# A normaliser that goes through DRAM: sixteen rows in place of eight

## The chip, the cores and the metric

The kernel runs on one core of a Trainium2 chip. The core has a matrix engine (TensorE, PE in the profile), a vector engine (VectorE, DVE), a scalar engine (ScalarE, ACT), GpSimd (POOL), and SyncE (SP), which here only issues transfers; the transfers themselves run on 16 DMA engines. The metric is the device time of one launch in microseconds (us). Several launches are timed and their median is taken.

## The reference

The input x is 2048 tokens by 512 features in bf16. Four layers follow one another, each added to x behind a layer norm: A, B, A, B.

```
q, k, v = split(layernorm(x) @ wqkv)                     # 32 heads of 16
A:  phi(u) = concat(softmax(u @ w_phi), softmax(-u @ w_phi))   # 32 features per head
    kv = sum over tokens of phi(k) (x) v,   z = sum over tokens of phi(k)
    o  = (phi(q) @ kv) / (phi(q) . z + 1e-6)
B:  o  = softmax over 8 earlier positions (step 2) of q.k / 4, applied to v
x = x + o @ wo
```

The change is in layer A. The query's features phi(q) are softmaxes, and the result is divided by a denominator: for each token, head and sign one number, the normaliser rho, carries the reciprocal of the softmax sum and the reciprocal of the denominator. The kernel multiplies the unnormalised exponentials of the query by it.

## The kernel before

The 2048 tokens are four blocks (b = 0 to 3) of 512 tokens; a block is four tiles (t) of 128. L = 0 and 1 is the pair of layers A and B. For each L the kernel runs `s_a1` (keys and values of layer A) and `s_a2` (queries) for the four blocks, `s_akv` (the summed kv), and then for each block `s_a3` (denominator and normaliser), `s_a4` (output, projection, residual and next layer norm), and `s_b1`, `s_b2`, `s_b3` for layer B.

Each step of a stage is put on a list of its engine, and a long written-out order (`_ORDER`, L57) says in which sequence the steps of all stages are emitted. Each engine takes its instructions strictly in that order, and so does SP: a transfer that has to wait holds up all transfers behind it on SP. Semaphores of the program stand wherever one engine needs another's result. Transfers take their completion semaphores from eight in turn.

In `s_a3` the engines make rho: the products with the denominators on PE (`md`), a product and a sum on DVE (`dr`, L790 and L793), a logarithm and an exponential on ACT (`ln`, L796 and L797), and rho itself on DVE (`rho`, L801). It is a tile of 128 partitions: 32 rows (heads) for each of the four token tiles, with two signs (s) of 128 tokens each. The exponentials `Eq` of the query, however, have a head's 16 features on 16 partitions, eight heads to a group of 128 partitions, so that each value of rho has to reach 16 partitions. For four of the eight blocks this is done by matmuls with a 0/1 matrix (`bc`, L808) and DVE products from PSUM (`mulp`, L816). For the other four, listed in `_OPT["rho_dma"]` as (0,2), (0,3), (1,2) and (1,3), it is done by DMA:

- `wr` (L824) writes rho to a DRAM buffer `rd` of 8 rows and two signs, one row for each head within a group; a row holds 16 pieces (four token tiles by four head groups) of 128 values, that is 4 KB.
- `rdb(s)` (L831), once for each sign, reads each of the 8 rows sixteen times, so that each of the 128 partitions of the tile `Prho` receives 4 KB: 512 KB in all.
- `muld(s)` (L835) is one DVE product of `Eq` and `Prho`, 128 by 2048 values, in place.

SP's order around the four places is: the write, the two reads, and then whatever transfer comes next. At block (0,3) the transposing transfer `xnT<-xn` (L451), which brings the layer-normed block (0,2) to layer B's projections on PE (L927), stands between the two reads. Behind the reads come the loads of the values' tiles, `Vg<-V` (L988), which DVE multiplies by the attention weights (`pav`, L1081).

Of the kernel before, what the change touches and what calls it, by code (L numbers as in the profile page):

```python
# [8 lines left out]
BF16 = mybir.dt.bfloat16  # L9
# [7 lines left out]
P = 128  # L17
# [112 lines left out]
class _Fast:  # L130
# [640 lines left out]
    def s_a3(self, L, b, dma):  # L771
        nc, add = self.nc, self.step
        st = "a3_%d%d" % (L, b)
        zm = self.ZM[L]
        T = {}
# [42 lines left out]
        pitch = (16 + _OPT["rho_pad"]) * P  # L818

        def wr():  # L820
            self.RD[L, b] = rd = self.dram.tile([8, 2, pitch], BF16, name="rd%d%d" % (L, b))
            a = rd[0:1, 0, 0:P]
            dst = bass.AP(a.tensor, a.offset, [[P, 16], [2 * pitch, 8], [pitch, 2], [1, P]])
            nc.sync.dma_start(out=dst, in_=T["rho"][:])  # L824

        def rdb(s):
            rd = self.RD[L, b]
            T["P", s] = pr = self.med([4, NB, P], "Prho")
            a = rd[0:1, s, 0:P]
            src = bass.AP(a.tensor, a.offset, [[2 * pitch, 8], [0, 16], [1, 16 * P]])  # L830
            nc.sync.dma_start(out=pr[:].rearrange("p t a i -> p (t a i)"), in_=src)  # L831

        def muld(s):
# [14 lines left out]
        if dma:  # L848
            add(st, "SP", wr)
            for s in range(2):  # L850
                add(st, "SP", rdb, s)
            for s in range(2):
                add(st, "DVE", muld, s)
            return
# [963 lines left out]
```

## Time and profile before

| what | value |
|---|---|
| median of 3 runs | 330.01 us (329.47 to 330.12) |
| span of the profiled execution, first to last instruction | 327.5 us |
| PE, DVE, ACT busy | 95%, 92%, 85% of the span |
| SP's queue (q1) | 36816 packets, 34.81 MB |
| HBM read, written | 10.50 MB, 2.36 MB |
| granted TensorE clock | 0.998 |

For the profiled execution the trace has the span alone, and no device time; the runs' median is 2.5 us above the span. A row of the timeline gives the start in us from the span's first instruction, the duration, engine, line, operation and tile; in brackets stands how long the engine was idle before and what ended that wait. A row of the windows gives a stretch of time, each engine's busy time in it with the number of instructions, the granted clock, the mean share of the 16 DMA engines that moved a packet (it can come out above 1 where an engine overlaps packets), and the rate in GB/s. The profile's own name for a transfer's issue is the line on SPq.

### The profile page before, as it was taken

What the parts mean: (1) busy time and instruction counts of PE and PEld (TensorE: products, weight loads), DVE (VectorE), ACT (ScalarE), POOL (GpSimd) and SP (SyncE); (2) the same over time, 40 slices, a digit from 0 to 9 for tenths busy, and PEclk for the clock granted to TensorE, in tenths of its full rate; (3) what the DMA queues carried; (4) which work ended last, traced back from release to release, by engine and by line L of the source; (5) the groups of instructions that cost most, each with busy time, mean ns of one, the idle gap of its engine ahead of it and who ended that gap; (6) DMA issues with size and microseconds to landing.
All of it is one profiled execution on the core that took longest, in us unless ns stands there. A gap on an engine that the chain in (4) does not pass through costs nothing. (4 is left out here: it accounts for less than half of the span.)

```text
span 327.5 us, 8033 instructions
## 1 busy us (share of the span) xinstructions
PE 310.3 (95%) x3176; PEld 149.5 (46%) x3203; DVE 302.2 (92%) x439; ACT 279.3 (85%) x634; POOL 25.3 (8%) x50
## 2 busy tenths in 40 slices
PE   7999999999999999999999999979999999999873
PEld 3655456445444444443444455644544454433221
DVE  7998995998998999899999999699999999999993
ACT  5999988998888999989999999798999996676550
POOL 4000000000021003000000000000000208400000
PEclk9999999999999999999999999999999999999999
DMA  7980000004556899998750300023436977679952
GB/s 197 380 197 3 0 2 4 2 20 120 105 148 135 152 164 133 139 121 154 137 135 1 67 3 2 4 59 90 128 58 125 179 146 134 150 139 158 166 176 92
DMA packets 37388, 35.41 MB, mean 108 GB/s; under 512 B 23008, under 2 KB 32224, under 8 KB 37344
## 3 DMA queue, kind: packets, MB, share of 16 engines
q1 hardware_dynamic: 36816, 34.81, 53.6%
q8 instruction: 27, 0.44, 0.6%
q14 instruction: 17, 0.14, 0.2%
q10 hardware_dynamic: 528, 0.02, 0.1%
HBM read 10.50 MB, written 2.36 MB: 39 GB/s over the span
## 5 line engine op out<-in xcount | busy, mean ns | idle before, releaser
L927 PE MATMUL ps<-xnT,WB 128*128 128x512 bf16 x384 | 87.6, 380 | 0.5 <-DMA xnT<-xn 0.5
L1081 DVE TENSOR_TENSOR pav<-PT,Vg 128x4096 bf16<-128x4096 bf16 (+1 forms) x34 | 72.0, 2162 | 1.5 <-DMA Vg<-V 1.0
L1019 DVE TENSOR_TENSOR prod<-QT,K 128x4096 bf16<-128x4096 bf16 x32 | 72.5, 2291 | 0.3 <-ACT QT L192 0.2
L927 PEld LDWEIGHTS <-WB 128*128 128x128 bf16 x384 | 42.3, 114 | 43.3 <-issue 5.8
L520 PEld LDWEIGHTS <-oT 128*128 128x128 bf16 x256 | 23.8, 97 | 34.5 <-ACT oT L192 5.7
L192 ACT CAST oT<-ps 128x512 bf16<-128x512 f32 (+1 forms) x60 | 32.1, 587 | 8.4 <-PE ps L1090 7.1
L706 ACT ACTIVATE Eq<-ps 128x512 bf16<-128x512 f32 x64 | 34.0, 615 | 0.7 <-PE ps L698 0.6
L520 PE MATMUL ps<-WoB,oT 128*128 128x512 bf16 x122 | 32.1, 380 | 2.4 <-ACT oT L192 2.0
L599 ACT ACTIVATE Ek<-ps 128x512 bf16<-128x512 f32 x64 | 33.6, 622 | 0.4 <-PE ps L593 0.2
L698 PE MATMUL ps<-xnT,WA 128*128 128x512 bf16 x128 | 30.7, 380 | 0.6 <-DVE Eq L816 0.6
L540 ACT ACTIVATE sqd<-x 128x512 bf16<-128x512 bf16 x48 | 30.1, 643 | 1.0 <-DVE x L533 0.8
L605 PE MATMUL ps<-WA,xnT 128*128 128x512 bf16 x120 | 30.0, 380 | 0.5 <-issue 0.2
L593 PE MATMUL ps<-WA,xnT 128*128 128x512 bf16 x124 | 29.7, 380 | 0.6 <-DMA xnT<-xn 0.2
L520 PE MATMUL ps<-WoA,oT 128*128 128x512 bf16 x120 | 29.2, 380 | 0.4
L533 DVE SCALAR_TENSOR_TENSOR x<-ps,x 128x512 bf16<-128x512 f32 x38 | 25.4, 686 | 1.9 <-PE ps L520 1.7
L192 ACT CAST V<-ps 128x512 bf16<-128x512 f32 x31 | 17.5, 595 | 4.4 <-PE ps L927 4.3
L192 ACT CAST K<-ps 128x512 bf16<-128x512 f32 x31 | 17.8, 585 | 3.7 <-PE ps L927 3.3
L530 ACT ACTIVATE x<-ps 128x512 bf16<-128x512 f32 x26 | 15.1, 598 | 6.4 <-PE ps L523 6.3
L192 ACT CAST QT<-ps 128x512 bf16<-128x512 f32 x29 | 17.1, 592 | 2.5 <-PE ps L927 2.5
L651 DVE TENSOR_TENSOR Ek<-Ek,rk 128x4096 bf16<-128x4096 bf16 (+1 forms) x10 | 18.6, 1858 | 0.5 <-ACT rk L646 0.5
L593 PEld LDWEIGHTS <-xnT 128*128 128x128 bf16 x128 | 12.1, 97 | 15.4 <-DMA xnT<-xn 0.7
L446 ACT ACTIVATE xn<-x,nmr,rstd 128x512 bf16<-128x512 bf16 x23 | 18.2, 822 | 1.0 <-DVE nmr L435 0.8
(129 smaller groups left out, 433.3 us busy)
## 6 DMA issues: line engine op xcount, KB each, us to landing
Vg<-V SPq DMA_DIRECT2D x128, 131.5 KB, 4.4
Prho<-rd SPq DMA_DIRECT2D x8, 512.0 KB
x<-in_A_x_dram SPq DMA_DIRECT2D x3, 512.0 KB
WB<-in_B_wqkv_dram SPq DMA_DIRECT2D x3, 512.0 KB, 11.6
wraw<-in_A_wqkv_dram SPq DMA_DIRECT2D x4, 256.0 KB, 4.5
out_dram<-x SPq DMA_DIRECT2D x4, 256.0 KB, 2.2
out_dram<-x SPq DMA_DIRECT2D x8, 128.0 KB, 2.2
x<-in_A_x_dram SPq DMA_DIRECT2D x4, 128.0 KB
```

What stands on the lines that cost most here:

```text
L192: self.nc.scalar.copy(out=out, in_=in_)
L520: nc.tensor.matmul(y[:], lhsT=oT[:, c, t * P:(t + 1) * P], rhs=Wo()[:, c, :], start=(c == 0), stop=(c == NB - 1 and not onpe))
L533: nc.vector.scalar_tensor_tensor(out=xb[:, t, :], in0=T[t][:], scalar=1.0, in1=xb[:, t, :], op0=ALU.mult, op1=ALU.add, **kw)
L540: nc.scalar.activation(out=sqd[:], in_=xb[:, t, :], func=ACT.Square, accum_out=T["ss"][:, t:t + 1])
L593: nc.tensor.matmul(pk[:], lhsT=xnT[:, t, k, :], rhs=self.WA[:, k, D:2 * D], start=(k == 0), stop=(k == NB - 1))
L599: nc.scalar.activation(out=T["E"][:, t, s, :], in_=T["k", t][:], func=ACT.Exp, scale=1.0 - 2.0 * s)
L605: nc.tensor.matmul(pv[:], lhsT=xnT[:, t, k, :], rhs=self.WA[:, k, 2 * D:3 * D], start=(k == 0), stop=(k == NB - 1))
L698: nc.tensor.matmul(pq[:], lhsT=self.WA[:, k, hb * P:(hb + 1) * P], rhs=xnT[:, :, k, :], start=(k == 0), stop=(k == NB - 1))
L706: nc.scalar.activation(out=self.Eq[L, b][s][:, :, hb, :], in_=T[hb][:].rearrange("p (t i) -> p t i", t=4), func=ACT.Exp, scale=1.0 - 2.0 * s)
L927: nc.tensor.matmul(pp[:], lhsT=self.WB[:, k, i * D + c:(i + 1) * D:NB], rhs=xnT[:, :, k, :], start=(k == 0), stop=(k == NB - 1))
L1019: nc.vector.tensor_tensor(out=pr[:], in0=QT[:, c:c + 1, :].to_broadcast([P, NW, TB]), in1=win, op=ALU.mult)
L1081: nc.vector.tensor_tensor(out=pv, in0=PT[:, :, lo:lo + n].unsqueeze(1).to_broadcast([P, NB, 2, n]), in1=vw, op=ALU.mult)
```

## The change

The DRAM buffer gets 16 rows: each of the 8 old rows stands in it twice, one copy beside the other. Two transfers write it, one for each sign, where one transfer wrote both signs; each writes its 64 KB half of the new buffer with rho's values read twice (the repeat is a zero step in the source's access pattern). Each read then goes through 16 rows and reads each eight times. The bytes and the destination of the reads are the same, and so is the order of all steps.

```diff
         def wr():
-            self.RD[L, b] = rd = self.dram.tile([8, 2, pitch], BF16, name="rd%d%d" % (L, b))
-            a = rd[0:1, 0, 0:P]
-            dst = bass.AP(a.tensor, a.offset, [[P, 16], [2 * pitch, 8], [pitch, 2], [1, P]])
-            nc.sync.dma_start(out=dst, in_=T["rho"][:])
+            self.RD[L, b] = rd = self.dram.tile([16, 2, pitch], BF16, name="rd%d%d" % (L, b))
+            for s in range(2):
+                a = rd[0:1, s, 0:P]
+                dst = bass.AP(a.tensor, a.offset, [[P, 16], [4 * pitch, 8], [2 * pitch, 2], [1, P]])
+                nc.sync.dma_start(out=dst, in_=T["rho"][:, s, :].unsqueeze(1).to_broadcast([P, 2, P]))
 
         def rdb(s):
             rd = self.RD[L, b]
             T["P", s] = pr = self.med([4, NB, P], "Prho")
             a = rd[0:1, s, 0:P]
-            src = bass.AP(a.tensor, a.offset, [[2 * pitch, 8], [0, 16], [1, 16 * P]])
+            src = bass.AP(a.tensor, a.offset, [[2 * pitch, 16], [0, 8], [1, 16 * P]])
             nc.sync.dma_start(out=pr[:].rearrange("p t a i -> p (t a i)"), in_=src)
```

## Prediction

> **What bounds the kernel now.** I read the page first, then the timeline of SP around the four places where rho goes through DRAM, then DVE's and PE's timelines there, and last the windows with the DMA share.
>
> ```profile
> span 327.5 us, 8033 instructions
> PE 310.3 (95%) x3176; PEld 149.5 (46%) x3203; DVE 302.2 (92%) x439; ACT 279.3 (85%) x634; POOL 25.3 (8%) x50
> ...
> q8 instruction: 27, 0.44, 0.6%
> ...
> PE 26%; DVE 3%; ACT 2%; issue 1%; DVEq 0%
> ```
>
> PE and DVE are both nearly full, and the last part of the span hangs on PE. A transfer counts only where one of the two stands still for it. So the question is whether anything waits for the write or the reads of rho, or for a transfer that stands behind them. SP's timeline has the issues (start, time of the issue):
>
> ```profile
> 69.39 0.58 SPq L824 DMA_DIRECT2D rd<-rho  x1
> 71.66 1.51 SPq L831 DMA_DIRECT2D Prho<-rd  x2
> 80.86 0.59 SPq L824 DMA_DIRECT2D rd<-rho  x1
> 83.10 0.57 SPq L831 DMA_DIRECT2D Prho<-rd  x1
> 87.06 3.03 SPq L451 DMA_TRANSPOSE xnT<-xn  x1
> 90.19 0.60 SPq L831 DMA_DIRECT2D Prho<-rd  x1
> ...
> 214.45 0.62 SPq L824 DMA_DIRECT2D rd<-rho  x1
> 216.66 1.38 SPq L831 DMA_DIRECT2D Prho<-rd  x2
> 224.04 0.59 SPq L824 DMA_DIRECT2D rd<-rho  x1
> 227.99 1.24 SPq L831 DMA_DIRECT2D Prho<-rd  x2
> 242.01 1.73 SPq L451 DMA_TRANSPOSE xnT<-xn  x1
> ```
>
> I call the places A (69.39), B (80.86), C (214.45) and D (224.04). In each, SP waits for the write to land before it issues the read. DVE's products with Prho:
>
> ```profile
> 81.11 1.23 DVE L835 TENSOR_TENSOR Eq<-Eq,Prho 128x2048 bf16<-128x2048 bf16 x1
> 82.78 1.22 DVE L835 TENSOR_TENSOR Eq<-Eq,Prho 128x2048 bf16<-128x2048 bf16 x1
> 96.03 2.39 DVE L835 TENSOR_TENSOR Eq<-Eq,Prho 128x2048 bf16<-128x2048 bf16 x2
> 100.25 0.69 DVE L190 CAST QT<-ps 128x512 bf16<-128x512 f32 x1 [0.99 <-PE ps L927]
> ...
> 226.75 1.22 DVE L835 TENSOR_TENSOR Eq<-Eq,Prho 128x2048 bf16<-128x2048 bf16 x1
> 228.22 1.22 DVE L835 TENSOR_TENSOR Eq<-Eq,Prho 128x2048 bf16<-128x2048 bf16 x1
> ```
>
> ```profile
> L835 DVE TENSOR_TENSOR Eq<-Eq,Prho x8: 1215/1220/1252, 81.1 to 240.0; 128x2048 bf16<-128x2048 bf16 x8
> ```
>
> No product has idle time before it: a timeline's row would name it in brackets, as that at 100.25 does, and the view of the tile Prho, from which the last row groups all eight, lists no wait. So they never wait for their reads, so reads that come sooner give nothing by themselves. The windows (length, busy time of PE, PEld, DVE, ACT and POOL, clock, DMA share, GB/s) show what the transfers do:
>
> ```profile
> 8.00:12.00 4.00, 3.77 (x62) 3.50 (x63) 3.95 (x10) 3.84 (x9) 0.38 (x1) 1.00 1.07 372
> ...
> 73.10:77.10 4.00, 4.00 (x90) 2.64 (x90) 2.96 (x12) 3.44 (x10) 0.00 (x0) 1.00 0.55 138
> 77.10:81.00 3.90, 3.85 (x20) 1.81 (x17) 3.63 (x10) 3.81 (x11) 0.00 (x0) 1.00 0.48 131
> 81.00:82.05 1.05, 1.05 (x6) 0.58 (x5) 1.04 (x2) 0.81 (x3) 0.00 (x0) 1.00 0.00 0
> 82.05:82.70 0.65, 0.65 (x4) 0.34 (x3) 0.61 (x3) 0.37 (x2) 0.00 (x0) 1.00 0.58 114
> 84.40:88.20 3.80, 3.80 (x48) 1.73 (x47) 3.80 (x4) 3.46 (x7) 0.15 (x1) 1.00 0.51 138
> ...
> 89.50:91.02 1.52, 1.52 (x9) 0.71 (x8) 0.89 (x4) 1.52 (x1) 0.00 (x0) 1.00 1.14 256
> 91.05:91.50 0.45, 0.45 (x4) 0.21 (x3) 0.45 (x1) 0.45 (x3) 0.00 (x0) 1.00 0.00 0
> ```
>
> A read of 512 KB takes 3.8 to 4.0 us, at a DMA share of about one half: 131 to 138 GB/s. The loads at 8 to 12 us ran at a share of 1.07 and 372 GB/s, so half is not what all transfers get. A share of one half says that eight of the 16 engines carry a read, or that all 16 are idle half the time; I take the first, as the reads go over eight rows.
>
> The Trainium skill, page "DMA: Bandwidth & Descriptors", section "Why a DMA increments its semaphore by 16 and not by 1", gives a rule for this: the number of engines is the largest one up to 16 that divides the slowest dimension of both access patterns, 8 here and 16 after the change. The share of 0.48 to 0.55 agrees.
>
> One wait in the neighbourhood does touch the path, and it is for the transpose at B:
>
> ```profile
> 93.12 7.10 PE L927 MATMUL ps<-xnT,WB 128*128 128x512 bf16 x32 [0.46 <-DMA xnT<-xn]
> DMA to landing us min/median/max: 4.3/4.6/4.6
> ```
>
> The second row is that of the tile xnT, for the transposes whose landing the trace has. The one at B was issued at 87.06 and PE resumed at 93.12, which is 6.06 us: some 1.5 us more than 4.6. PE lost 0.46 us by it, and seven microseconds later DVE lost 0.99 us to PE (the row at 100.25).
>
> **The change part by part.**
>
> *The write.* A second transfer of the same kind and count of 256-byte pieces comes behind the first: 0.59 us more on SP (median of the four write rows above), four times, 2.4 us in all, none on PE or DVE. If each read depends on its own sign's write alone, the second issue lies inside the wait of the first: 71.66 − 69.39 − 0.58 = 1.7 us of SP's idle time. The first read then keeps its place, and the second needs a write landed 0.6 us later than the first, when SP comes to it 0.75 us after the first read. If both writes must land before the first read, it moves by about 0.6 us. If the second write also waits for the first (both go to one buffer, and the trace of before cannot show how the dependency is drawn), the read moves by another landing, 71.66 − 69.39 = 2.3 us. I take the first, as the two halves don't overlap, and keep 2.3 us as the bad end. On the DMA engines the second write costs what the first does (82.05 to 82.70, 0.65 us), a gap in which nothing else moves.
>
> The Trainium skill's page "DMA: Bandwidth & Descriptors", section "Specifications", speaks against this part: under 512 B a transfer is a read-modify-write and not at full rate, and the change doubles the 256-byte pieces. By the page the write could only get dearer; by the row it is 0.65 us of otherwise empty engine time.
>
> *The reads.* With 16 engines at the rate that each has now, a read takes half: 1.9 to 2.0 us (ends: 3.9, no gain; and 512 KB at the 372 GB/s of the window at 8 us, 1.4). At A both would be done at about 77, where they end at 81.0 now. First use is at 81.11 and 82.78: gain 0. At C they end some 4 us earlier and at D more, as D's write no longer queues behind C's reads (224.04 to 227.99 is 3.95 us for a landing that takes 2.2 to 2.3 elsewhere). No DVE row there waits, and SP's next transfer is the transpose at 242.01, held by its data: gain 0. What hides all this is DVE's and PE's own work; if DVE were to come to its products 4 us sooner, the old reads would show.
>
> *The transpose at B.* The first read's packets now run to about 88.2, into the transpose issued at 87.06; its issue took 3.03 us, where the one at 242.01 with empty engines took 1.73. Read in 2 us from 84.4, the engines are empty at 86.4, before the transpose. The second read, issued behind it, follows on the same engines and cannot overtake. So I expect the transpose to land within 4.6 us, at 91.7. PE is then ready at 93.12 − 0.46 = 92.66, and the wait is gone: −0.46 us. The bounds are 0 (the lateness has another cause: the last two windows show the data over at 91.02, two microseconds before PE resumes, and one late packet of the instruction queue q8 on one engine would explain that) and −0.46 (beyond it PE waits for its own work). I take −0.46, since the delayed issue is the odd thing in the row, and a transpose that ends a little earlier also misses such a packet.
>
> Does it carry? DVE's wait of 0.99 at 100.25 is for these very matmuls, so DVE receives it; its next wait is for a transfer of Vg, once:
>
> ```profile
>   DMA Vg<-V: 1.0, 1
> ```
>
> Those loads start behind layer-norm work that moves along. I count it in full.
>
> *Sum.* Write 0, reads 0, transpose −0.46: the span goes from 327.5 to 327.0. The runs' median stands 2.5 us above the span; I leave that as it is: 330.01 − 0.46 = 329.55 us. No change within 0.2% (0.66 us, about what a measurement of this kernel can tell) could be told from it.
>
> **The rivals.**
>
> *The wait stays.* Either the reads are no faster (all 16 engines were at half load, and the row count means nothing), or the transpose is late for the instruction packet. For it: the two microseconds after 91.02. Against it: the share of just one half. Time 330.0.
>
> *The second write waits for the first (the other side).* Then B's first read moves from 83.10 to 85.4 and its data from 84.4 to 86.7. With a read of 1.95 us the engines are free at 88.65, 0.45 later than 88.2 now, and PE waits that much longer: 330.5. With a read that still takes 3.9 us they are free at 90.6 and PE loses 2.4: 332.4. It decides from a read of about 2.2 us on, where the loss passes 0.66. For it: one buffer and one queue in order. Against it: the written halves are disjoint.
>
> *All 16 engines full.* Reads on every engine leave none free for the small transfers that now slip past on the other eight, such as instruction packets; a fetch that is late stops an engine. The price is bounded by the 2 us of one read in the worst place; I take 1 us: 331.0. The same reshuffle can also clear another chance wait, DVE's 1.0 for Vg: 329.0. For it: PE and DVE have no slack. Against it: the reads are few (8) and get shorter.
>
> **How the numbers follow.** Forecast 45% (36 within 0.2%; 9 faster by more, where DVE's 0.99 closes wholly). The wait stays: 23%, all within. Serial writes: 15% (11 slower, 4 within). All engines full: 17% (11 slower, 6 faster). Together faster 15%, same 63%, slower 22%. The forecast's own range is 329.2 to 330.0. The range for 8 in 10 goes from 329.0, the lucky reshuffle, to 331.0, the unlucky one, and leaves out the serial writes with slow reads.
>
> **What would show it.** In the changed kernel's windows the reads at A have a share near 1 and 260 to 270 GB/s, and end near 77; the write has two rows on SP 0.6 us apart, and the first read follows the first write by 2.3 us; B's transpose issues in about 2 us and PE's row at L927 has no wait for xnT; the products of L835 have no idle time before them. Wrong would be: a share that stays at one half (rows don't set the engines), a gap of 2.3 us between the two writes (they are serial), or new idle time of PE or DVE put down to xnT, Prho or an issue.

## The result, and the profile after

The changed kernel takes 328.65 us (median of 16 runs, 328.06 to 329.63), the kernel before on the same chip 329.54 us (16 runs, 328.36 to 330.49). The ratio is 0.9973, with a 95% interval from 0.9961 to 0.9985: 0.9 us faster, between 0.5 and 1.3. A second series gave 328.70 against 329.88, ratio 0.9969 (0.9956 to 0.9983). One run of a later version (first read wide at B) took 811.51 us, and its ratio leaves that run out.

In every execution recorded with both numbers the device time is about 1.7 us above the span. The 2.5 us given ahead of the prediction compare a median with the span of another execution, which was a faster one than the median (327.5 + 1.7 = 329.2).

The page of the changed kernel, in the lines that answer to those of before:

```profile
span 326.7 us, 8039 instructions
PE 310.7 (95%) x3176; PEld 149.7 (46%) x3203; DVE 302.2 (92%) x439; ACT 279.3 (85%) x634; POOL 25.5 (8%) x50
...
q8 instruction: 27, 0.44, 0.6%
...
HBM read 10.50 MB, written 2.62 MB: 40 GB/s over the span
```

The engines' busy times are those of before; the written bytes grew by the four doubled buffers. SP's issues around the four places:

```profile
69.71 1.25 SPq L825 DMA_DIRECT2D rd<-rho  x2
71.96 1.28 SPq L832 DMA_DIRECT2D Prho<-rd  x2
81.17 1.22 SPq L825 DMA_DIRECT2D rd<-rho  x2
83.40 0.54 SPq L832 DMA_DIRECT2D Prho<-rd  x1
87.37 1.90 SPq L451 DMA_TRANSPOSE xnT<-xn  x1
89.38 1.09 SPq L832 DMA_DIRECT2D Prho<-rd  x1
...
223.61 1.22 SPq L825 DMA_DIRECT2D rd<-rho  x2
225.78 1.91 SPq L832 DMA_DIRECT2D Prho<-rd  x2
```

The two writes go out back to back (1.22 to 1.25 us for both), and the first read still follows the first write by 2.2 to 2.3 us, so the second write does not hold it up. The windows (columns as before) at A and at B:

```profile
73.40:75.40 2.00, 2.00 (x10) 0.75 (x8) 1.17 (x7) 1.69 (x6) 0.00 (x0) 1.00 0.96 264
75.40:77.60 2.20, 2.15 (x82) 1.98 (x83) 1.90 (x7) 1.96 (x4) 0.00 (x0) 1.00 0.93 218
...
84.70:86.70 2.00, 2.00 (x40) 0.79 (x38) 2.00 (x3) 1.66 (x4) 0.15 (x1) 1.00 0.92 256
86.70:88.50 1.80, 1.80 (x11) 0.92 (x9) 1.80 (x2) 1.80 (x4) 0.00 (x0) 1.00 0.06 11
```

The share went from one half to 0.92 to 0.96, the rate from 131 to 138 GB/s to 256 to 264 (218 in the second window, which is longer). The trace also records each packet, and there a read has a tail: from its first packet to its last it takes 2.2 to 2.9 us, and 3.4 us for the one behind the transpose at B, where it took 3.9 to 4.2, once 5.2. The same records count the engines: each read of before ends with eight packets of 4 bytes, each read of the changed kernel with sixteen, which I take for one per engine.

At B the engines are nearly empty from 86.7 on. The last packet of the read ends at 87.25, just before the transpose is issued at 87.37, and the issue takes 1.90 us where it took 3.03. PE's and DVE's timelines behind it:

```profile
90.22 2.75 PE L520 MATMUL ps<-WoA,oT 128*128 128x512 bf16 x12
92.81 7.07 PE L928 MATMUL ps<-xnT,WB 128*128 128x512 bf16 x32
```

```profile
96.34 2.39 DVE L836 TENSOR_TENSOR Eq<-Eq,Prho 128x2048 bf16<-128x2048 bf16 x2
99.92 0.69 DVE L190 CAST QT<-ps 128x512 bf16<-128x512 f32 x1 [0.34 <-PE ps L928]
```

PE no longer waits for xnT, and DVE's wait for PE shrank from 0.99 to 0.34. No other wait of PE or DVE between A and this place moved by more than 0.01 us.

**A measure that leaves out the start.** The first instructions of DVE's work on A come at 68.9 to 71.0 us in the executions of this study, and the time varies between executions of one kernel. So the profiles are compared from the start of rho at A. "To B's product" runs from there to the start of DVE's product (L1019, L1020 or a shifted line) that follows the cast of QT near 100 us; "to PE's end" runs from there to the end of PE's last matmul.

| kernel | rho at A | to B's product | PE's wait for xnT | to PE's end |
|---|---|---|---|---|
| before, first profile | 68.94 | 31.92 | 0.46 | 253.24 |
| before, again | 69.28 | 32.01 | 0.55 | 253.38 |
| before, third profile | 68.98 | 32.05 | 0.59 | 253.36 |
| changed | 69.26 | 31.26 | none | 252.49 |
| changed, again | 69.85 | 31.27 | none | 252.53 |

The change gives 0.65 to 0.79 us up to B's product, and all of it is still there at PE's end (0.71 to 0.89).

### The profile page after: what moved, and what is told of

It is laid out like the page before. It is cut to its first block, busy times and chain, and to the rows that moved or that the text cites. A ratio compares the mean times of both kernels' runs of the same rounds, so it can differ in the third digit from the quotient of the medians.

```text
span 326.7 us, 8039 instructions
## 1 busy us (share of the span) xinstructions
PE 310.7 (95%) x3176; PEld 149.7 (46%) x3203; DVE 302.2 (92%) x439; ACT 279.3 (85%) x634; POOL 25.5 (8%) x50
## 4 chain that ended last, share of the span: by engine, by line
PE 77%; ACT 7%; DVE 6%; DMA 4%; issue 3%; SPq 2%; DVEq 0%
PE ps L928 23%; PE ps L520 14%; PE ps L593 9%; PE ps L605 8%; PE ps L698 6%; PE ps L1027 4%; PE ps L1091 3%; DVE prod L1020 3%; DMA Vg<-V 3%; PE ps L668 2%; ACT oT L192 2%; PE ps L460 2%; ACT Eq L706 2%; DMA wraw<-in_A_wqkv_dram 1%; PE ps L901 1%
## 5 line engine op out<-in xcount | busy, mean ns | idle before, releaser
L1020 DVE TENSOR_TENSOR prod<-QT,K 128x4096 bf16<-128x4096 bf16 x32 | 72.5, 2291 | 0.3 <-ACT QT L192 0.2
L1091 PE MATMUL ps<-pav,indAV 128*32 128x512 bf16 (+1 forms) x272 | 17.7, 370 | 1.2 <-DVE pav L1082 1.1
```

Source lines behind the costliest of these rows:

```text
L1020: nc.vector.tensor_tensor(out=pr[:], in0=QT[:, c:c + 1, :].to_broadcast([P, NW, TB]), in1=win, op=ALU.mult)
L1091: nc.tensor.matmul(po[32 * c:32 * c + 32, lo:lo + n], lhsT=self.indAV[:], rhs=T["p", q][:, c, hf, lo:lo + n], start=(hf == 0), stop=(hf == ...
```

## Which place and which read

**The change at B alone.** In each of the two functions the new form is taken for one block and the old one for the rest:

```diff
-        def wr(): ...
+        if (L, b) == (0, 3):
+            (wr and rdb as changed: sixteen rows)
+        else:
+            (wr and rdb as before: eight rows)
```

> The change at block (0,3) alone (place B), the other three places as before. Both theories that put the gain at B, the one on the read in front of the transpose and the one on the instruction packet behind it, expect the whole gain here: about 0.9 us less than before (ratio 0.997), and no wait of PE for xnT near 93 us. The rival that the gain is spread over the four places expects a quarter of it, 0.2 us (0.9993), with the wait at B gone or not.

Measured: 329.22 us against 330.05, ratio 0.9972 (0.9960 to 0.9984). In its profile it is 31.27 us to B's product, and PE does not wait. To PE's end it is 252.89 us, so that 0.35 to 0.49 us of the gain at B are left there. So the change at B is enough to end the wait; what the other places give, the next version tells.

**The change everywhere but at B**, the same with `(L, b) != (0, 3)`.

> The change at (0,2), (1,2) and (1,3), place B as before. Theories with the gain at B expect the time of before (ratio 1.000, at most 0.1%) and PE's wait of some 0.5 us for xnT near 93 us still there. The rival of a gain spread over the places expects three quarters of it, 0.7 us (0.998).

Measured: 329.56 against 330.05, ratio 0.9975 (0.9963 to 0.9988). That is the time that the rival of a gain spread over the places expected (0.998), and not the time of before. The profile says the opposite: PE waits at B as before,

```profile
93.61 7.10 PE L943 MATMUL ps<-xnT,WB 128*128 128x512 bf16 x32 [0.58 <-DMA xnT<-xn]
```

with 32.04 us to B's product and 253.35 to PE's end, nothing gained. The same kernel in a second series:

> The change at (0,2), (1,2) and (1,3) alone, a second time. Its first timing said 0.25% less than before, while its profile had the wait at B and the stretch from place A to the end of PE 0.1 us longer than before. If places A, C and D give something that the profiles do not show, the ratio is 0.9975 again; if the first timing was off, it is 1.000 within 0.1%.

329.34 against 329.88, ratio 0.9984 (0.9973 to 0.9996): smaller, but not 1.000. Either the wait is sometimes missing, or the start is shorter in some executions; two more profiles of this kernel and one of the kernel before:

> One more profile of the change at (0,2), (1,2) and (1,3) alone. If its smaller times come from executions in which the wait at B is missing, this profile or the next lacks PE's wait near 93 us and is 0.65 us shorter there; if they come from the start, place A is reached earlier than in the profiles of the kernel before; if neither, the gain at these places stays unexplained.

> A second look at the change at (0,2), (1,2) and (1,3) alone, with the same three outcomes: the wait near 93 us missing (0.65 us less there), place A reached earlier, or neither.

> One more profile of the kernel before: the wait at B again if it is in every execution, and the time at which place A is reached, as the third sample of the start.

Neither. In all four profiles of this kernel PE waits for xnT (0.58, 0.50, 0.73 and 0.54 us), rho at A starts at 69.3 to 70.1, no earlier than in the kernel before (68.9 to 69.3), and PE's end is at 253.35 to 253.73. What its timed runs gain (0.8 and 0.5 us by the two ratios) no profile shows, and it stays open. So the times alone do not place the gain: what the change gains at B alone (0.9972) and everywhere else (0.9975, 0.9984) adds up to more than the whole change gains (0.9973, 0.9969). What is shown is what the profiles show: PE's wait at B ends with the change at B.

**The kernel before against itself.**

> The kernel before, unchanged, timed against itself: all theories expect a ratio of 1.000. How far it falls from that, and where its profile differs from the first one from start to place A and from there to the end, says how small a difference these comparisons can tell. PE's wait of about 0.5 us for xnT near 93 us should be there again, if it belongs to the kernel and not to one execution.

329.69 against 329.70, ratio 1.0006 (0.9991 to 1.0020). A difference of 0.15% is about the least that one series can tell. PE's wait is there again (0.55 us).

**The second copy without the wider read.** Both writes are as changed, but each read goes over every other row:

```diff
-            src = bass.AP(a.tensor, a.offset, [[2 * pitch, 16], [0, 8], [1, 16 * P]])
+            src = bass.AP(a.tensor, a.offset, [[4 * pitch, 8], [0, 16], [1, 16 * P]])
```

> Sixteen rows written by two transfers, but each read goes over eight of them, sixteen times each. The theory that the number of rows in the read sets the engines expects reads of about 4 us at a DMA share of one half, and no gain: the time of before (1.000) or up to 0.2% more. If the second copy or the second write brought the gain, it would be here: 0.9 us less (0.997).

Measured: 329.58 against 330.05, ratio 0.9990 (0.9973 to 1.0007). The reads at A are as slow as before, and end with eight packets of 4 bytes, although the buffer has sixteen rows:

```profile
73.40:77.40 4.00, 4.00 (x91) 2.58 (x89) 3.08 (x12) 3.44 (x11) 0.00 (x0) 1.00 0.42 134
```

PE waits 0.44 us, and it is 31.91 us to B's product. So the outer count of the read's access pattern sets the engines here, and the extra write costs nothing that can be measured.

**One read at a time at B.** Sixteen rows are written at block (0,3) only, and one of its two reads uses them all:

```diff
+                rows = ([[2 * pitch, 16], [0, 8], [1, 16 * P]] if s == 0
+                        else [[4 * pitch, 8], [0, 16], [1, 16 * P]])
+                src = bass.AP(a.tensor, a.offset, rows)
```

> At block (0,3) sixteen rows are written and only the first read, which runs into the transpose, goes over all of them; the second read goes over eight. The theory that the first read holds up the transpose's issue expects the whole gain of place B: the issue of the transpose in about 2.0 us, its last landing within 4.8 us, no wait of PE, 0.65 us less from place A to the end of PE than before. The rival (the second read, or the copy) expects the wait to stay.

> The counterpart: at block (0,3) only the second read, which is issued behind the transpose, goes over sixteen rows; the first goes over eight. The first-read theory expects no gain: the transpose issues in 2.9 to 3.0 us, PE waits about 0.5 us for xnT, and the stretch from place A to the end of PE is that of before within 0.2 us. The rival expects 0.65 us less.

The first read wide: 329.06 against 329.70, ratio 0.9976 (0.9961 to 0.9990), 31.26 us to B's product. The second read wide: 329.80, ratio 1.0001 (0.9989 to 1.0014), 32.17 us. The lines of SP and PE, first read wide and then second read wide:

```profile
87.90 2.05 SPq L451 DMA_TRANSPOSE xnT<-xn  x1
...
93.34 7.07 PE L944 MATMUL ps<-xnT,WB 128*128 128x512 bf16 x32
```

```profile
87.53 2.92 SPq L451 DMA_TRANSPOSE xnT<-xn  x1
...
93.83 7.10 PE L944 MATMUL ps<-xnT,WB 128*128 128x512 bf16 x32 [0.70 <-DMA xnT<-xn]
```

One of the eight reads makes the whole gain at B: the one in front of the transpose, whose packets run into its issue on eight rows.

**Eight rows, with the first read behind the transpose.** The tile is taken at its old place, and both reads of block (0,3) are issued where the second was:

```diff
         def rdb(s):
+            rd_alloc(s)
+            if (L, b) != (0, 3):
+                rd_load(s)
+            elif s == 1:
+                rd_load(0)
+                rd_load(1)
```

> Eight rows as before, but at block (0,3) the first read is issued behind the transpose, together with the second. If a read in front is what makes the transpose late, its issue falls from 3.0 to about 2 us, its last landing comes within 4.8 us, and PE no longer waits for xnT near 93 us, though nothing is read over sixteen rows. The price is visible too: the second read then ends some 4 us later, at about 99.5, and DVE should wait some 2 us for it before its product at 97. If the wait of PE stays, the read in front is not the cause.

One run, 336.05 us. SP, PE and then DVE:

```profile
87.26 2.14 SPq L451 DMA_TRANSPOSE xnT<-xn  x1
...
92.69 7.07 PE L938 MATMUL ps<-xnT,WB 128*128 128x512 bf16 x32
```

```profile
96.66 1.23 DVE L846 TENSOR_TENSOR Eq<-Eq,Prho 128x2048 bf16<-128x2048 bf16 x1 [0.36 <-DMA Prho<-rd]
103.96 1.23 DVE L846 TENSOR_TENSOR Eq<-Eq,Prho 128x2048 bf16<-128x2048 bf16 x1 [6.07 <-DMA Prho<-rd]
```

With no read in front, the transpose issues in 2.14 us and PE does not wait, on eight rows. The price was put at some 2 us of DVE's wait and is 6.07. A window of the same profile shows the first read by itself:

```profile
91.30:95.40 4.10, 4.10 (x21) 2.08 (x19) 4.10 (x8) 3.77 (x13) 0.00 (x0) 1.00 0.52 125
```

That is 512 KB in 4.1 us, much as in the kernel before. The second read follows it from 95.4 on, beside the loads of Vg that SP issues from 95.47 on (8.94 us for eight of them), and DVE has it only at 103.96, more than 8 us later. The cover that hides these reads is real, and it is thin.

## Why the transpose was late: an instruction packet

At B the long issue goes with the read in front, but that does not yet explain PE's wait. The following is read from the records of each packet and of each completion count, which the views shown here add up. The transpose completes in 16 counts. All times are us from its issue at B; "packet" is the 16 KB packet of the instruction queue q8 that comes nearest to its end.

```
kernel                    issue  data ends  15th count  16th count  packet from..to
before                     3.03   3.97        4.42        6.02       3.97..4.92
before, again              3.06   4.10        4.56        6.11       4.08..5.03
change at A, C, D only     2.90   4.12        4.55        6.14       4.14..5.08
sixteen rows, narrow read  2.90   3.96        4.36        6.00       3.95..4.90
second read wide           2.92   4.17        4.62        6.26       4.15..5.11
changed                    1.90   4.08        4.48        4.77       4.09..5.04
changed, again             1.88   3.99        4.41        4.63       4.00..4.94
change at B only           2.03   4.05        4.63        4.75       4.06..5.01
first read wide            2.05   4.06        4.63        4.75       4.06..5.01
reads behind, eight rows   2.14   4.02        4.56        4.63       4.03..5.05
```

The data of the transpose are no later with a long issue: they end at 3.96 to 4.17 us in all ten rows. Fifteen counts are there at 4.4 to 4.6 us, soon enough that PE would not wait. In the five late kernels the sixteenth comes 1.6 us later. In all ten rows the instruction packet starts as the data end. The records do not name the engine of a packet, but they show which came first: each transpose has 32 packets of 4 bytes, two for each count, at the end of its data. In the kernel before, 30 of them end by 3.97, and the last two end at 4.93, with the instruction packet (to 4.92). In the changed kernel all 32 end by 4.09, where the packet starts. It is the same in the other rows: the last two end at 4.91 to 5.13 in the late kernels and by 4.09 in the others. So on one engine the instruction packet stands between the data and their completion. That accounts for about 1 us; the sixteenth count then comes 1.1 us behind its 4-byte packets, where the fifteen others take about 0.4 to 0.7, and this part of the lateness is not explained.

At B the packet came first wherever the issue was long, and the completion wherever it was short. The Trainium skill has the two pieces: the page "Runtime: NRT & Kernel Launch", section "Instruction fetch mechanics", says that instructions are fetched in blocks of 16 KiB over DMA queues of their own, and calls the cost mostly hidden; the page "DMA: Bandwidth & Descriptors", section "Queues, rings and completion order", says that a DMA engine takes turns between queues packet by packet. The packet of 16 KB and the order of the 4-byte packets agree with both. But the cost is not hidden here: it falls on the transfer that the packet cuts in on.

This can be tested without touching the rows: a different number of instructions on PE ahead of B moves the fetches against the work. The kernel warms PE with 14 matmuls on a zero tile at the start; their result isn't used.

```diff
         def warm():
             ...
+            self.nwarm = getattr(self, "nwarm", 0) + 1
+            if self.nwarm > 10:
+                return
             nc.tensor.matmul(self.warm_ps[:], lhsT=self.kvT[:, 0:P], rhs=self.kvT[:], start=True, stop=True)
```

> The kernel before with 10 in place of 14 warming matmuls on PE at the start, so that PE's instruction stream is eight instructions shorter and its 16 KB fetches fall some 0.9 us later against the work. The packet theory (the transpose at B is late because an instruction packet of q8 sits on one engine as it ends) expects PE's wait for xnT near 93 us to go, with eight rows as before, and 0.5 to 0.9 us less (about 0.9975), unless the start itself gets longer. The read theory (the transpose is late because of the read in front) expects the wait to stay and the time of before.

Measured: 331.14 against 330.05, ratio 1.0042 (1.0021 to 1.0062), against the packet theory's expectation. The packet did not move away: it starts 4.12 us after the issue, again just as the data ends, the sixteenth count is at 6.25, and PE waits 0.70 us. A fetch that is asked for at a somewhat different time may still be held until the same end of data; no record shows when it was asked for. So this run settles nothing between the theories. In its profile the loss lies at the start (rho at A at 70.30) and at a later transposing transfer, for which PE waits 0.57 us at 151.10. The other direction, 18 matmuls in all (with 13 in place of 5, 26 in all):

```diff
+            self.nwarm = getattr(self, "nwarm", 0) + 1
-            nc.tensor.matmul(self.warm_ps[:], lhsT=self.kvT[:, 0:P], rhs=self.kvT[:], start=True, stop=True)
+            for _ in range(5 if self.nwarm == 1 else 1):
+                nc.tensor.matmul(self.warm_ps[:], lhsT=self.kvT[:, 0:P], rhs=self.kvT[:], start=True, stop=True)
```

> Four matmuls more on PE at the start: PE's 16 KB fetches then fall eight instructions, some 0.9 us, earlier against the work. With eight rows. In every profile with the wait at B so far, 15 of the transpose's 16 completions came 4.4 to 4.6 us after its issue and the last at 6.0 to 6.3, behind one instruction packet of q8. If the packet makes the wait, moving it may clear it: the last completion then comes by 5.6 us and PE does not wait. If the long issue alone makes it, PE waits its 0.5 us as before.

> Twelve matmuls more on PE at the start, fetches some 2.6 us earlier, eight rows. The packet theory expects the packet of q8 in the first half of the transpose or ahead of it, the last completion within 5.6 us and no wait of PE for xnT near 93 us, with the issue of the transpose as long as before (2.9 to 3.0 us). The theory that the read in front does it alone expects the wait to stay.

Eight rows, as before, with 18 and with 26 matmuls, one profile each. SP and PE with 18:

```profile
87.63 3.21 SPq L453 DMA_TRANSPOSE xnT<-xn  x1
...
93.07 7.07 PE L929 MATMUL ps<-xnT,WB 128*128 128x512 bf16 x32
```

The issue is as long as ever, 3.21 us, and PE does not wait. The packet of q8 now runs from 0.33 to 1.53 us after the issue, ahead of the transpose's data, and the sixteenth count is at 4.60 (with 26 matmuls 4.40). To B's product it is 31.27 us in both, the figure of the changed kernel. The wait at B goes away without a change of rows or reads, and to PE's end it is 252.63 with 18 and 253.12 with 26.

> The changed kernel with four matmuls more at the start, fetches 0.9 us earlier. The packet theory expects that the wait can come back here: if the packet now gets ahead of the transpose's last completions, the last comes at some 6 us and PE waits about 0.5 us near 93 us, though the reads are as short as in the changed kernel. The read theory expects no wait.

> The changed kernel with twelve matmuls more at the start, fetches 2.6 us earlier. Both theories expect no wait for xnT near 93 us; the packet theory because the packet is then served ahead of the transpose's end. From place A to the end of PE within 0.2 us of the changed kernel, unless another fetch meets another transfer.

The changed kernel has no wait at B with either (31.27 and 31.26 us). That the wait could come back with 18 was not seen: the packet had passed already. But with 26 the gain is lost elsewhere, at another transposing transfer, here PE in the changed kernel with 26:

```profile
186.06 0.81 PE L595 MATMUL ps<-WA,xnT 128*128 128x512 bf16 x3 [0.61 <-DMA xnT<-xn]
```

and the issue of that transfer:

```profile
179.79 2.00 SPq L453 DMA_TRANSPOSE xnT<-xn  x1
```

This issue is short, and the records have no other transfer's data beside it. Yet the instruction packet (3.98 to 4.90 us after the issue) comes ahead of the last two 4-byte packets, which end at 4.92, and the sixteenth count is at 6.00. The same transfer in the other kernels with 18 or 26 matmuls also meets a packet, which starts at 3.96 to 4.00, with an issue of 1.9 to 2.0 us as well; there the completion goes first, and the sixteenth count is at 4.62 to 4.70. So a short issue does not make sure that the completion goes first. What tips the order is not shown.

To PE's end it is 253.24 us with 26, as in the kernel before. The kernel before with 18 was also timed, beside the changed kernel:

> Eight rows and four matmuls more on PE at the start, timed. In its profile the wait at B was gone without any change of the rows, 0.6 us less from place A to the end of PE, and the start some 0.2 us later than most. The packet theory expects 0.9980 to 0.9990; if the time is that of before (1.000), the profile's gain is lost at the start.

> The changed kernel once more, on the same chip as the others here. Its profile should again lack the wait at B, with the stretch from place A to the end of PE some 0.7 us shorter than in the first profile of before, and the ratio should be 0.997 to 0.998, if the 0.65 us at B is all there is (0.9980) or if some more comes with it (0.9973).

The kernel before with 18 warming matmuls: 329.36 against 329.88, ratio 0.9987 (0.9975 to 1.0000), with 31.27 us to B's product once more. The changed kernel: 328.70, ratio 0.9969. The time of the first is in the range that the packet theory expected, though its interval just reaches 1; it falls short of the changed kernel, and no version here has a lower ratio than the changed kernel.

## Why the prediction was right or wrong

**The direction and the place were right.** The write costs nothing that can be measured, the faster reads by themselves end no wait, and the wait that goes is PE's for the transpose at B. The share of the reads (0.92 to 0.96), the back-to-back writes, the first read 2.2 to 2.3 us behind the first write, the transpose's issue of 1.9 us, and D's write that no longer queues behind C's reads (223.61 to 225.78, where it was 3.95 us) came as forecast. The reads are not quite halved: to their last packet they take 2.2 to 2.9 us, and at A they end at 78.0, not near 77. At B that left only 0.12 us between the end of the read and the transpose. Serial writes did not happen, and no new wait for xnT, Prho or an instruction packet shows in the changed kernel's profiles.

**The size was wrong.** 0.46 us was forecast; at B it is 0.66, and the time fell by 0.9 (0.5 to 1.3), to 328.65, below the range's lower end of 329.0. The step that failed is the bound on the transpose, "beyond it PE waits for its own work". The idle time in a PE row understates what a wait costs. A matmul row lasts 380 ns, but the rows follow one another every 0.21 to 0.22 us: twelve take 2.75 us in the row at 90.22 above. The changed kernel's next matmul starts at 92.81, 0.16 us before that row's end at 92.97. In the kernel before, the tail was over when the wait of 0.46 began. So the loss was about 0.46 + 0.16 = 0.62 us, and DVE's row says nearly the same: its wait fell by 0.99 − 0.34 = 0.65. The prediction had DVE's 0.99 in hand and took PE's smaller number.

**That it carries was right.** 0.66 us at B's product and 0.75 at PE's end, first profile against first profile; nothing behind it took it back. With the change at B alone 0.35 of it is left at PE's end.

**The reason was half of it.** The prediction took the late landing for a matter of the long issue, with the instruction packet as the way in which it might be wrong, and it noted that an earlier end could miss such a packet. The packet is needed for the wait: with 18 matmuls the issue is as long, on eight rows, and there is no wait. The read in front is needed too: with the packet at the same place, a read that is short or moved behind leaves no wait at B. How the read puts the packet ahead of the completion is not shown. It is not by later data, and not by the length of the issue alone, as the transfer at 179.79 shows. The rival "the wait stays" rested on the packet and fell because at B the completion came ahead of it. There was some luck in that.

**The rest of the time is not settled.** The runs gained 0.9 and 1.0 us by the two ratios; the profiles account for 0.65 to 0.79 at B's product, which lies within both intervals, so that a rest is not shown. But the kernel with the change at the other three places gained time in two series, and no profile of it shows where. The median of the kernel before also came out lower than in the three runs that the forecast started from, 329.54 against 330.01; these 0.47 us are half of the distance between 329.55 and 328.65, and they come from which runs were taken and not from the change.

## What to carry to other kernels

It can pay to put a count of 16 outermost in a transfer's access pattern, even at the price of writing a copy: here that about doubled the rate of eight reads. Seven of them gave nothing that a profile shows, and the eighth no longer ran into the next transfer. Where an engine waits for a transfer whose data had ended long before, look in the packet records for an instruction packet on one of the engines; a few instructions more or less elsewhere can move it, and such a gain belongs to one version of the program and not to its design. Price a wait of PE by the start of the next matmul against the spacing of those before it, or by the engine that waits for PE, not by the idle time of its row.

## What the runs showed of the hardware

- A 512 KB read with an outer count of 8 ended with eight 4-byte packets and ran at 131 to 138 GB/s; with 16 it ended with sixteen and ran at 256 to 264 GB/s in its first 2 us.
- The transposing transfer at B took 2.8 to 3.2 us to issue while an eight-engine read was still moving, and 1.9 to 2.1 us with the engines empty. The changed kernel with 18 warming matmuls took 3.2 us as well, with an instruction packet at 0.28 to 1.59 us after the issue.
- Where one 16 KB instruction packet, 0.95 us long, came between the data of the transpose and the 4-byte packets behind them, the last of 16 completions was 1.6 us later than the others, and with it the whole transfer.
- A read on eight engines took 4.1 us alone and more than 8 us beside the Vg loads.
